# Mixer weights from 64-bit words: signs on GpSimd, group scales and norms by TensorE, new buffer choice

## The chip, the cores and the metric

The kernel runs on one core of one Trainium2 chip. The metric is the device time of one execution in microseconds (us), taken several times; beside it stands one profiled execution, whose trace gives the duration of each instruction. The engines are named as in the profile: PE is TensorE (matmuls), DVE VectorE, ACT ScalarE, POOL GpSimd, SP SyncE, which issues most DMA transfers.

## The reference, cut to what matters

Eight batches, 8 heads, 576 positions, head width 64. Attention is computed twice, once over positions pooled in fours and once in a band of seven positions, and the sum goes through a two-stage mixer, over tokens and over channels.

```python
x = attention_pooled(q, k, v) + attention_band(q, k, v)   # (8, 576, 512)
xt = x.transpose(0, 2, 1)
h = np.maximum(xt @ w_tok1, 0.0) @ w_tok2                 # 576 -> 256 -> 576
u = x + h.transpose(0, 2, 1)
h2 = np.maximum(u @ w_ch1, 0.0) @ w_ch2                   # 512 -> 1536 -> 512
return u + h2
```

The four weights arrive as 64-bit floating-point numbers, and the kernel makes them usable itself, once, while the first batch runs.

## The kernel before, in words

Each batch goes through the same steps. `pooled` (four pairs of heads: products sd, transposes td, products ad) and `local` (five tiles of positions: scores sc, transposes pT, products av) are the attention. `mix` is the token mixer: it splits x into two halves xh, multiplies by W1 (t1), splits the result (hid), multiplies by W2 with x added by transposing matmuls (t2), takes the largest magnitude (umx, and `everywhere`: a reduce um_m, a transpose um_t, a reduce um_m1, a broadcast um_b) and scales u into fp16 pairs uh. `first` is the channel mixer's first product (c1, twelve tiles for each of two chunks of 256 and 320 columns, three matmul passes each), `first_up` makes h of it, and `second` is the second product (c2). The columns of a batch's `second` and the next batch's attention and token mixer are interleaved.

The weights go through `to_f32` tile by tile. A raw tile has a high and a low 32-bit word for each element. ACT scales the high words (L175), POOL turns the low words into a small number (L178), DVE joins the two in one pass over two inputs (L180), and a second DVE pass, in `signed` (L184), puts the sign in and writes the tile to its place. For the token weights (W, nine tiles) ACT copies the upper part and DVE subtracts it (L215). For the channel weights (C1 and C2, twelve tiles of 128x512 each) PE multiplies the raw tiles by ones (C_sum, L279 and L288), DVE reduces (L283), and one scale comes out of all twelve tiles of a weight (`big`, `pow2`, L262); only then ACT writes the fp16 upper half of each tile (L268) and DVE the lower half (L270), which every product of `first` needs:

```python
    yield step("V", 0.6, *([("C1", NF - 1)] if self.at else []))
    nc.vector.tensor_reduce(big, self.mx[:, :self.n], axis=AX.X, op=ALU.max)
    pow2(big, 2.0 ** -self.k, self.inv, self.s)
```

Raw tiles of W and C1 share five buffers (`h`), those of C2 come in pairs in the two buffers `vw`. At the start POOL builds three masks and a pattern with many small selections, and adds the value rows (vr, L344 and L345) for the pooled attention.

The order of all this for the first batch, the weights and the first steps of the second batch is made by the list scheduler `drive`: streams yield steps with an engine, an assumed duration and needs, and the step that can begin earliest is written next (within PATIENCE, 0.3 us, the earlier stream wins). From the second batch on `main` writes a batch's channel products, and `tick` lets the next batch's other work (`side`) in between them at a fixed rate.

## Time and profile before

| what | value |
|---|---|
| runs | 975.58 to 978.17 us, median 976.34 of 3 |
| profiled execution | 977.24 us |
| its span, first to last instruction | 975.5 us |
| busy in the span | PE 907.9, DVE 506.0, ACT 301.1, POOL 112.4 us |
| granted TensorE clock, mean | 0.975 of full speed |

The profiled execution lies 0.90 us above the median, and its span 1.74 us below its own time. PE is busy 93% of the span, DVE 52%; these are means over stages with different limits. The first 110 us hold the attention and token mixer of batch 0 and most of the weights' preparation, and the rest is eight times the channel mixer with the next batch's other work in between. The profile's line for 40 equal slices shows PE at 5, 7, 4, 7, 7 tenths in the first five slices, and at 8 or 9 from there on.

### The profile page before, as it was taken

Reading aid. Unit: us, or ns where it says so; the run is one execution under the profiler, and the core shown is the slowest. Engines: PE = TensorE matmul, PEld = TensorE weight load, DVE = VectorE, ACT = ScalarE, POOL = GpSimd, SP = SyncE. Lnnn points to the kernel's source line nnn. Section 1 sums busy time; section 2 is a strip of 40 time slices with the busy share of each in tenths; the row PEclk is TensorE's granted clock in tenths of the full one; section 3 lists DMA queues with packets and bytes.
Section 4 is the critical chain, followed back from the end, with each engine's and each line's share of the span. In section 5 each row is a group of like instructions: output and inputs, shape, how many; then the busy total and the mean of one; then the engine's idle time right before and its main releaser. Section 6 shows DMA issues by size and latency. Waiting matters only on the chain. (4 is left out here: it accounts for less than half of the span.)

```text
span 975.5 us, 25542 instructions
## 1 busy us (share of the span) xinstructions
PE 907.9 (93%) x11292; PEld 712.2 (73%) x11292; DVE 506.0 (52%) x1187; ACT 301.1 (31%) x627; POOL 112.4 (12%) x213
## 2 busy tenths in 40 slices
PE   5747789999999999999999999999999999999998
PEld 4634467778867778677877778777876778777876
DVE  7879899244645354724555354724645345533221
ACT  1544456212323232422333232422432222322110
POOL 7143500030030003000120003000120000000000
PEclk9976799999999999999999999999999999999999
DMA  8266610530025002500133002600034000000000
GB/s 225 96 234 239 217 31 2 159 90 21 26 61 158 22 8 76 168 7 21 38 107 100 15 14 72 171 1 28 20 84 140 15 15 20 18 2 21 18 12 28
DMA packets 28221, 68.28 MB, mean 70 GB/s; under 512 B 3504, under 2 KB 14000, under 8 KB 26864
## 3 DMA queue, kind: packets, MB, share of 16 engines
q1 hardware_dynamic: 25552, 64.30, 21.9%
q10 hardware_dynamic: 2560, 2.36, 0.9%
q8 instruction: 88, 1.44, 0.6%
q14 instruction: 21, 0.17, 0.1%
HBM read 54.85 MB, written 9.44 MB: 66 GB/s over the span
## 5 line engine op out<-in xcount | busy, mean ns | idle before, releaser
L105 PEld LDWEIGHTS <-CW 128*128 128x128 f16 x4608 | 435.7, 98 | 136.5 <-issue 15.3
L105 PE MATMUL c<-uh,CW 128*128 128x256 f16 (+1 forms) x2304 | 310.7, 288 | 7.0 <-DVE CW L270 4.4
L105 PE MATMUL c<-h,CW 128*128 128x256 f16 (+1 forms) x2304 | 304.5, 287 | 0.8 <-issue 0.7
L646 DVE SCALAR_TENSOR_TENSOR h<-c,h 128x256 f16<-128x256 f32 (+1 forms) x192 | 87.3, 455 | 133.0 <-ACT h L644 131.9
L644 ACT ACTIVATE h<-c 128x256 f16<-128x256 f32 (+1 forms) x192 | 78.4, 408 | 211.2 <-PE c L105 211.0
L344 POOL TENSOR_TENSOR vr<-vr 72x256 f32<-72x256 f32 x64 | 49.0, 765 | 489.4 <-DMA vr<-in_vr_dram 298.1
L672 DVE SCALAR_TENSOR_TENSOR u<-c,io,u 128x256 f32<-128x256 f32 (+1 forms) x64 | 33.0, 516 | 109.7 <-PE c L105 109.7
L554 DVE TENSOR_REDUCE umx<-t 128x1 f32<-128x256 f32 (+1 forms) x64 | 29.2, 457 | 84.5 <-ACT u L552 84.4
L105 PE MATMUL t<-W,hid 128*128 128x256 f32 (+1 forms) x384 | 71.6, 323 | 0.0
L105 PE MATMUL t<-xh,W 128*128 128x512 f32 (+1 forms) x240 | 68.2, 419 | 1.1 <-ACT x L480 0.8
L552 ACT COPY u<-t 128x256 f32<-128x256 f32 (+1 forms) x64 | 25.5, 398 | 119.9 <-PE t L105 119.6
L105 PEld LDWEIGHTS t<-W,hid 128*128 128x128 f32 x384 | 56.7, 200 | 2.6 <-DVE hid L531 0.3
L105 PEld LDWEIGHTS t<-xh,W 128*128 128x128 f32 (+1 forms) x240 | 43.6, 192 | 12.5 <-issue 2.5
L475 PE MATMUL av<-vw,pt 47*32 47x64 f32 x2304 | 37.1, 233 | 14.6 <-ACT pt L466 4.4
L480 ACT COPY x<-av 128x512 f32<-128x512 f32 (+1 forms) x40 | 23.3, 582 | 88.4 <-PE av L475 80.9
L475 PEld LDWEIGHTS av<-vw,pt 47*32 47x32 f32 x2304 | 28.9, 110 | 25.2 <-issue 11.4
L567 ACT ACTIVATE uh<-u,us 128x256 f16<-128x256 f32 (+1 forms) x64 | 29.6, 524 | 49.0 <-DVE us L111 45.0
L407 PE MATMUL ad<-vd,ptd 72*72 72x65 f32 x512 | 42.5, 240 | 0.1
L407 PEld LDWEIGHTS ad<-vd,ptd 72*72 72x72 f32 x512 | 40.5, 157 | 1.3 <-ACT ptd L401 0.4
L545 PEld LDWEIGHTS t<-ident,x 128*128 128x128 f32 (+1 forms) x160 | 22.4, 146 | 18.4 <-issue 9.1
L545 PE MATMUL t<-ident,x 128*128 128x128 f32 (+1 forms) x160 | 33.0, 287 | 2.3 <-DVE umx L554 2.3
L569 DVE SCALAR_TENSOR_TENSOR uh<-u,us,uh 128x256 f16<-128x256 f32 (+1 forms) x64 | 31.1, 537 | 7.6 <-ACT uh L567 7.6
(84 smaller groups left out, 802.6 us busy)
## 6 DMA issues: line engine op xcount, KB each, us to landing
qk<-in_qk_dram SPq DMA_DIRECT2D x32, 579.0 KB
vw<-in_vw_dram SPq DMA_DIRECT2D x32, 351.0 KB
vr<-in_vr_dram SPq DMA_DIRECT2D x64, 144.0 KB
C_raw<-in_c_dram SPq DMA_DIRECT2D x12, 512.0 KB
C_raws<-in_c_dram SPq DMA_DIRECT2D x12, 512.0 KB
out_dram<-u SPq DMA_DIRECT2D x32, 160.0 KB
out_dram<-u SPq DMA_DIRECT2D x32, 128.0 KB
vw<-od ACTq DMA_DIRECT2D x32, 72.0 KB
```

The costliest lines, as they stand in the source:

```text
L105: nc.tensor.matmul(ps, lhs(a), rhs(c), start=first and i == 0, stop=last and i == 2, **kw)
L344: nc.gpsimd.tensor_add(t[:, 0:2], t[:, 0:2], t[:, 2:4])
L407: nc.tensor.matmul(ps[:, g, par], pt[:, par, kg, G * g:G * g + G], st.vd[:, kg, 2 * pr + par], start=kg == 0, stop=kg == 1)
L475: nc.tensor.matmul(ps[QB * j:QB * j + QB, par, D * hp:D * hp + D], pt[p, hp, QB * j:QB * j + QB], st.vw[h][p, g, D * hp:D * hp + D], start ...
L545: nc.tensor.matmul(ps[:, o:o + n], xf(t)[:, 128 * c:128 * c + 128], ident[:n, :n], start=i == 0, stop=False, is_transpose=True, skip_group ...
L552: nc.scalar.copy(u, ps)
L554: nc.vector.tensor_reduce(umx[:, c:c + 1], ps, axis=AX.X, op=ALU.max, apply_absolute_value=True)
L567: nc.scalar.activation(t[:, 0], us[c], AF.Copy, scale=s)
L569: nc.vector.scalar_tensor_tensor(t[:, 1], us[c], s, t[:, 0], ALU.mult, ALU.subtract)
L644: nc.scalar.activation(ht[:, 0], ps, AF.Relu)
L646: nc.vector.scalar_tensor_tensor(ht[:, 1], ps, 0.0, ht[:, 0], ALU.max, ALU.subtract)
L672: nc.vector.scalar_tensor_tensor(us[c], banks[c], io, us[c], ALU.mult, ALU.add)
```

## The change

- **Signs.** `to_f32` has a second POOL instruction per tile (L214, behind the first, now L211): it takes the high words and writes the upper 16 bits of the sign into the low word. DVE's one pass (L219) then joins shifted high word and low word and writes the tile to its place; `signed` is gone. SG=4 gives all 33 tiles' signs to POOL.
- **Norms and scales.** PE multiplies each finished tile by itself (L304 for C1, L323 for C2) in place of the product of ones and raw tile. C1 gets a scale for every four tiles (`First.scale`), so that the parts of a group (now L293) wait for that group alone. C2 has one scale, worked out from group norms that are multiplied by C1's constants (`Second.scale`).
- **Loads and buffers.** C1's raw tiles have six buffers of their own (`cw`, later C2's finished tiles), W's the five of `h`; C2's first four raw tiles use batch 0's `qk` buffers, the rest the pairs in `vw`. PSUM banks and the buffers `w` have a tag each, and `drive` picks the one that comes free first.
- **PE filler.** `keep_busy` writes matmuls of a constant tile, 14 at the start, and up to 8 ahead of a PE step for which the scheduler foresees a wait, until the second chunk's uh of batch 0; 88 of them stand ahead of batch 0's first c1 product, 22 of these ahead of the first sd.
- **Masks.** 10 selections and two copies in place of 26 and 8 selections; the pattern comes from a DVE reduce of the identity.
- **Mixer.** `mix` is four streams (splits, products, takes, scaled), which `together` interleaves with the next batch's attention start; `drive` runs until batch 0 is over and batch 1's first uh is made.

```diff
-PATIENCE = 0.3
+SG = 4
+PATIENCE = 0.0
...
+    def slot(k):
+
+        if not driven[0]:
+            now_in[k] = (now_in[k] + 1) % SLOTS[k]
+        return k + str(now_in[k])
...
-        return psum.tile([128, 512], F32, tag="m", name=name, bufs=3)
+        return psum.tile([128, 512], F32, tag=slot("m"), name=name, bufs=1)
...
+    for kind, j, base, step_ in ((0, 0, -3, 1), (2, 1, QB + 2, -1)):
+        nc.gpsimd.tensor_copy(masks[kind], m)
+        select(masks[kind][QB * j:QB * j + QB], base, 0, step_, WB, NEG)
...
+    def keep_busy(n):
+
+        if n:
+            ps = P1("busy")
+            for _ in range(n):
+                nc.tensor.matmul(ps, junk[:, :128], junk, start=True, stop=True)
...
+            if e == "P" and ("uh", 0, 1) not in made and free["g"]:
+                keep_busy(min(8, int((t - clock["P"]) * 0.6 / 0.22)))
...
+                i = now_in[k] = min(free[k], key=free[k].get)
+                del free[k][i]
...
+        top = raw.bitcast(BF16).rearrange("p (n four) -> p n four", four=4)[:, :, 1]
...
         nc.gpsimd.tensor_scalar(lo, lo, 2.0 ** -29, -0.501, ALU.mult, ALU.add)
-        yield step("V", 0.08 + n * 0.0012)
-        nc.vector.scalar_tensor_tensor(lo, hi, 3, lo, ALU.logical_shift_left, ALU.bitwise_or)
...
-    def signed(y, raw):
-        words = raw.rearrange("p (n two) -> p n two", two=2)
-        nc.vector.scalar_tensor_tensor(y, words[:, :, 1], 0x80000000, words[:, :, 0],
-                                       ALU.bitwise_and, ALU.bitwise_or)
...
+        if by_pool():
+            yield step("G", 0.08 + n * 0.0026)
+            nc.gpsimd.tensor_scalar(top, hi.bitcast(F32), 2.0 ** -126, 2.0 ** -126, ALU.mult, ALU.mult)
+        else:
+            yield step("V", 0.08 + n * 0.0015)
+            nc.vector.scalar_tensor_tensor(lo, hi, 0x80000000, lo, ALU.bitwise_and, ALU.bitwise_or)
+        e = yield step("V", 0.08 + n * 0.0012, *needs)
+        nc.vector.scalar_tensor_tensor(lo if y is None else y(), hi, 3, lo, ALU.logical_shift_left, ALU.bitwise_or)
+        return e
...
+    def weight_loads(pieces, tag, name):
         raws = {}
...
         for i, (src, n) in enumerate(pieces):
...
+            yield step("S", 0.1, *([(name, "read", i - BUFS[tag])] if i >= BUFS[tag] else []))
+            raws[i] = T([src.shape[0], 2 * n], U32, tag, f"{name}{i}_raw")
+            nc.sync.dma_start(raws[i], src)
+            made[name, "raw", i] = fetched(src.shape[0] * n * 8)
+            made[name, "raw"] = raws
...
+        def tile(self, i, *needs):
             name = self.name
...
+            yield step("A", 0.0, (name, "raw", i))
+            raw = made[name, "raw"][i]
+            e = yield from to_f32(raw, made[name, "raw", i], lambda: self.place[i + 1].bitcast(U32), *needs)
+            make((name, "read", i), e)
+            e = yield step("P", 0.5, *([(name, "y", i - 1)] if i else []), take="m>" + name if i % 4 == 0 else "")
+            make((name, "y", i), e)
+            self.sums(i, self.place[i + 1].bitcast(BF16).rearrange("p (n two) -> p n two", two=2)[:, :, 1])
...
+        def norms(self, q):
+
+            yield step("V", 0.68, (self.name, "y", 4 * q + 3), give="m>" + self.name)
+            nc.vector.tensor_reduce(self.mx[:, q:q + 1], self.banks[q], axis=AX.X, op=ALU.max)
+
+        def root(self, src, f, inv, s):
+
+            nc.vector.tensor_scalar(inv.bitcast(U32), src.bitcast(U32), 0x7F000000, 1, ALU.bitwise_and,
+                                    ALU.logical_shift_right)
+            nc.vector.tensor_scalar(inv, inv, 2.0 ** 64 * f, 2.0 ** -60 * f, ALU.mult, ALU.max)
+            nc.vector.reciprocal(s, inv)
...
+    class First(Channel):
+        def sums(self, i, ab):
+
+            if i % 4 == 0:
+                self.banks[i // 4] = PM(f"C1_sum{i}")
+            for d in range(4):
+                a = ab[:, 128 * d:128 * d + 128]
+                nc.tensor.matmul(self.banks[i // 4][:, 128 * (i % 4):128 * (i % 4) + 128], a, a, start=d == 0, stop=d == 3)
+
+        def scale(self):
+            for q in range(NQ):
+                yield from self.norms(q)
+                big = yield from everywhere(f"C1_n{q}", self.mx[:, q:q + 1])
+                e = yield step("V", 0.45, give="g")
+
+                self.root(big, 2.0 ** (4.5 + 0.5 - 8), self.inv[q], self.s[q])
+                make(("C1", "scale", q), e)
+                for i in range(4 * q, 4 * q + 4):
+                    yield from self.parts(i)
...
+            big = yield from everywhere("C2_n", self.mx)
+            yield step("V", 0.9, give="g")
+
+            self.root(big, 2.0 ** (4.5 + 2 + 0.5 - 14), ic, self.s[0])
+            for q in reversed(range(NQ)):
+                nc.vector.tensor_mul(self.s[q], self.s[0], C1.inv[q])
...
+        def loads(self):
+
+            self.raws = made["C2", "raw"] = []
             for i in range(NF):
...
+                if i < 4:
+                    yield step("S", 0.1, *(("tile", 0, t) for t in range(len(TILES))))
+                    t = T([128, S + KW], F32, "qk", f"C2_raw{i}")[:, :1024].bitcast(U32)
+                else:
+                    if i % 2 == 0:
+                        yield step("S", 0.1, *(("av", 0, t) for t in range(len(TILES))), *([("C2", "read", i - 4), ("C2", "read", i - 3)] if i >= 8 else []))
+                        two = T([128, 2, 1024], U32, "vw", f"C2_raws{i}")
+                    t = two[:, i % 2]
+                nc.sync.dma_start(t, u32(c2[i]))
+                self.raws.append(t)
+                made["C2", "raw", i] = fetched(2 ** 19)
...
-    def sums_c1(w, i, ab):
-
-        if i % 4 == 0:
-            w.bank = PM(f"C1_sum{i}")
-        for d in range(4):
-            nc.tensor.matmul(w.bank[:, 128 * (i % 4):128 * (i % 4) + 128], onesb, ab[:, 128 * d:128 * d + 128],
-                             start=d == 0, stop=d == 3)
...
-            yield step("V", 0.6, *([("C1", NF - 1)] if self.at else []))
-            nc.vector.tensor_reduce(big, self.mx[:, :self.n], axis=AX.X, op=ALU.max)
-            pow2(big, 2.0 ** -self.k, self.inv, self.s)
...
+        return [splits(), products(), takes(), scaled()]
...
             m = mix(st)
             if b + 1 < B:
-                yield from together([m, ahead(b + 1)], 2)
-            else:
-                yield from m
+                m.append(ahead(b + 1))
+            yield from together(m, len(m))
...
+        keep_busy(14)
...
+        streams = [x for k in "LMUSCTDWmPaAHQh" for x in group[k]]
+        left = drive(streams, [("over", 0, 1)] + [("uh", 1, 0)] * (B > 1))
```

`parts` is the old loop of upper and lower halves, with the scale of the tile's group.

Where the instructions stand is shown at three places. The first is POOL, from its first weight tile (W10 and W0 are the first tile of W1, C10 the first of C1; W20 is the first of W2 before). Before:

```order
L178 TENSOR_SCALAR W10_raw_244<-W10_raw_244 128x256
L178 TENSOR_SCALAR C10_raw_248<-C10_raw_248 128x512
L178 TENSOR_SCALAR W11_raw_246<-W11_raw_246 128x256
L178 TENSOR_SCALAR W20_raw_253<-W20_raw_253 128x288
L178 TENSOR_SCALAR W12_raw_522<-W12_raw_522 128x256
L178 TENSOR_SCALAR W13_raw_711<-W13_raw_711 128x256
L178 TENSOR_SCALAR W21_raw_255<-W21_raw_255 128x288
L178 TENSOR_SCALAR C11_raw_250<-C11_raw_250 128x512
```

After the change, from the same point:

```order
L211 TENSOR_SCALAR W0_raw_199<-W0_raw_199 128x256
L214 TENSOR_SCALAR W0_raw_199<-W0_raw_199 128x256
L211 TENSOR_SCALAR C10_raw_207<-C10_raw_207 128x512
L211 TENSOR_SCALAR W1_raw_209<-W1_raw_209 128x256
L214 TENSOR_SCALAR C10_raw_207<-C10_raw_207 128x512
L214 TENSOR_SCALAR W1_raw_209<-W1_raw_209 128x256
L211 TENSOR_SCALAR C11_raw_211<-C11_raw_211 128x512
L211 TENSOR_SCALAR W2_raw_213<-W2_raw_213 128x256
L214 TENSOR_SCALAR C11_raw_211<-C11_raw_211 128x512
L214 TENSOR_SCALAR W2_raw_213<-W2_raw_213 128x256
```

Each tile has two instructions in place of one, and W's and C1's tiles alternate. 28 such pairs (8 of W, 20 of 128x512) stand between C10's L211 and the last raw tile whose join stands on DVE ahead of the first c1 product.

The second place is DVE ahead of what batch 0's first c1 product waits for. Before, that is the lower half CW0 of C1's first tile (the last row shown is the row ahead of it and one more):

```order
L569 SCALAR_TENSOR_TENSOR uh0_1_0_1267<-u0_1_0_1170,us0_1_1258,uh0_1_0_1267 128x320
L262 TENSOR_REDUCE C1_big_1269<-C1_mx_252 128x1
L109 TENSOR_SCALAR C1_inv_1270<-C1_big_1269 128x1
L110 TENSOR_SCALAR C1_inv_1270<-C1_inv_1270 128x1
L111 RECIPROCAL C1_s_1271<-C1_inv_1270 128x1
L569 SCALAR_TENSOR_TENSOR uh0_1_1_1274<-u0_1_1_1196,us0_1_1258,uh0_1_1_1274 128x320
L184 SCALAR_TENSOR_TENSOR CW22_198<-C28_raws_1109 128x512
L569 SCALAR_TENSOR_TENSOR uh0_1_2_1281<-u0_1_2_1213,us0_1_1258,uh0_1_2_1281 128x320
L270 SCALAR_TENSOR_TENSOR CW0_176<-CW1_177,C1_s_1271,CW0_176 128x512
L569 SCALAR_TENSOR_TENSOR uh0_1_3_1286<-u0_1_3_1235,us0_1_1258,uh0_1_3_1286 128x320
```

After, it is the last uh of the first chunk (the last row here); CW0 to CW7 are done, and CW8 and CW9 too:

```order
L282 TENSOR_SCALAR C1_inv2_123<-C1_n2_b_1337 128x1
L284 TENSOR_SCALAR C1_inv2_123<-C1_inv2_123 128x1
L285 RECIPROCAL C1_s2_126<-C1_inv2_123 128x1
L648 SCALAR_TENSOR_TENSOR uh0_0_1_1340<-u0_0_1_1174,us0_0_1309,uh0_0_1_1340 128x256
L219 SCALAR_TENSOR_TENSOR CX3_1179<-C2_raws6_1026 128x512
L293 SCALAR_TENSOR_TENSOR CW8_142<-CW9_143,C1_s2_126,CW8_142 128x512
L648 SCALAR_TENSOR_TENSOR uh0_0_2_1360<-u0_0_2_1201,us0_0_1309,uh0_0_2_1360 128x256
L219 SCALAR_TENSOR_TENSOR CX4_1180<-C2_raws6_1026 128x512
L293 SCALAR_TENSOR_TENSOR CW9_143<-CW10_144,C1_s2_126,CW9_143 128x512
L648 SCALAR_TENSOR_TENSOR uh0_0_3_1374<-u0_0_3_1221,us0_0_1309,uh0_0_3_1374 128x256
```

Ahead of the first c1 product DVE now has 29 passes L219 where it had 31 L180 and 31 L184; it has ten lower halves (L293) where it had one (L270), four of uh (of the first chunk) where it had seven (four of the first, three of the second chunk), and three group chains where there was one for all twelve tiles.

The third place is DVE where batch 1 ends and batch 2 begins (u1_1 is batch 1's output of its second chunk, the others belong to batch 2's mixer). Before:

```order
L488 TENSOR_REDUCE um2_0_m_4226<-umx2_0_4114 128x1
L672 SCALAR_TENSOR_TENSOR u1_1_2_2910<-c2_1_1_2_4174,io1_1_4034,u1_1_2_2910 128x320
L494 TENSOR_REDUCE um2_0_m1_4230<-um2_0_t_4228 1x1
L109 TENSOR_SCALAR ui2_0_4234<-um2_0_b_4232 128x1
L110 TENSOR_SCALAR ui2_0_4234<-ui2_0_4234 128x1
L111 RECIPROCAL us2_0_4235<-ui2_0_4234 128x1
L569 SCALAR_TENSOR_TENSOR uh2_0_0_4252<-u2_0_0_4124,us2_0_4235,uh2_0_0_4252 128x256
L569 SCALAR_TENSOR_TENSOR uh2_0_1_4255<-u2_0_1_4147,us2_0_4235,uh2_0_1_4255 128x256
L569 SCALAR_TENSOR_TENSOR uh2_0_2_4258<-u2_0_2_4173,us2_0_4235,uh2_0_2_4258 128x256
L569 SCALAR_TENSOR_TENSOR uh2_0_3_4261<-u2_0_3_4209,us2_0_4235,uh2_0_3_4261 128x256
L554 TENSOR_REDUCE umx2_1_4264<-t2_2_1_0_4265 128x1 x2
```

After:

```order
L751 SCALAR_TENSOR_TENSOR u1_1_1_2964<-c2_1_1_1_4276,io1_1_4192,u1_1_1_2964 128x320
L629 TENSOR_REDUCE umx2_1_4422<-t2_2_1_0_4326 128x1 x2
L751 SCALAR_TENSOR_TENSOR u1_1_2_2991<-c2_1_1_2_4336,io1_1_4192,u1_1_2_2991 128x320
L629 TENSOR_REDUCE umx2_1_4422<-t2_2_1_2_4373 128x1 x2
L557 TENSOR_REDUCE um2_0_m1_4442<-um2_0_t_4440 1x1
L551 TENSOR_REDUCE um2_1_m_4486<-umx2_1_4422 128x1
L118 TENSOR_SCALAR ui2_0_4449<-um2_0_b_4447 128x1
L119 TENSOR_SCALAR ui2_0_4449<-ui2_0_4449 128x1
L120 RECIPROCAL us2_0_4450<-ui2_0_4449 128x1
L648 SCALAR_TENSOR_TENSOR uh2_0_0_4471<-u2_0_0_4241,us2_0_4450,uh2_0_0_4471 128x256
L751 SCALAR_TENSOR_TENSOR u1_1_3_2997<-c2_1_1_3_4408,io1_1_4192,u1_1_3_2997 128x320
L648 SCALAR_TENSOR_TENSOR uh2_0_1_4477<-u2_0_1_4289,us2_0_4450,uh2_0_1_4477 128x256
```

Both reduces of the second chunk (umx2_1) have moved ahead of the first chunk's scale, and batch 1's last output u1_1_3 now stands between uh2_0_0 and uh2_0_1. On PE, um2_0_b has 57 matmuls behind it ahead of the first c1 of batch 2 before, and 9 now; for batches 3 to 6 these are 110 to 140 before and 22 to 26 now.

## Rows read from the trace of the kernel before

**Rows 1.** Stages: PE, PEld, DVE, ACT, POOL busy (instructions), clock, DMA share, GB/s.

```profile
29.20:110.20 81.00, 52.13 (x654) 37.79 (x652) 67.58 (x134) 35.38 (x74) 23.90 (x34) 0.78 0.57 206
110.20:171.00 60.80, 54.32 (x714) 40.52 (x715) 57.74 (x122) 34.76 (x65) 13.73 (x17) 0.93 0.15 33
...
200.00:975.50 775.50, 757.13 (x9216) 597.09 (x9214) 349.27 (x857) 216.28 (x464) 57.19 (x101) 1.00 0.17 49
```

**Rows 2.** PE's timeline: start, duration, instruction, idle before and releaser.

```profile
110.20 0.61 PE L105 MATMUL c<-uh,CW 128*128 128x256 f16 x2 [2.31 <-ACT CW L268]
112.30 2.74 PE L105 MATMUL c<-uh,CW 128*128 128x256 f16 x12 [1.49 <-DVE CW L270]
```

**Rows 3.** DVE's waits from 29.2 to 110.2: total us, times, longest.

```profile
DVE umx L554 <- ACT u L552: 3.9, 2, 2.8
DVE W_raw L180 <- POOL W_raw L178: 3.4, 2, 3.0
DVE hid L531 <- ACT hid L529: 2.0, 1, 2.0
```

**Rows 4.** DVE's groups by form in the same stretch: count, busy, mean ns.

```profile
L184 DVE SCALAR_TENSOR_TENSOR CW<-C_raw 128x512 uint32<-128x512 uint32 x12 | 9.4, 781 | 0.2
L180 DVE SCALAR_TENSOR_TENSOR C_raw<-C_raw 128x512 uint32<-128x512 uint32 x12 | 9.0, 752 | 0.9 <-POOL C_raw L178 0.9
...
L184 DVE SCALAR_TENSOR_TENSOR W_raw<-W_raw 128x288 uint32<-128x288 uint32 x4 | 1.8, 454 | 0.1
...
L569 DVE SCALAR_TENSOR_TENSOR uh<-u,us,uh 128x320 f16<-128x320 f32 x2 | 1.1, 541 | 0.0
```

**Rows 5.** DVE's timeline in stretches where POOL does nothing.

```profile
62.52 0.69 DVE L180 SCALAR_TENSOR_TENSOR C_raws<-C_raws 128x512 uint32<-128x512 uint32 x1
...
126.36 0.74 DVE L270 SCALAR_TENSOR_TENSOR CW<-CW,C_s,CW 128x512 f16<-128x512 f32 x1
```

**Rows 6.** POOL's timeline around its first weight tiles.

```profile
12.80 0.72 POOL L344 TENSOR_TENSOR vr<-vr 72x256 f32<-72x256 f32 x1
13.60 0.46 POOL L345 TENSOR_TENSOR vd<-vr 72x128 f32<-72x128 f32 x1
...
27.24 0.42 POOL L178 TENSOR_SCALAR W_raw<-W_raw 128x256 uint32<-128x256 uint32 x1 [6.98 <-DMA W_raw<-in_w_dram]
29.15 0.64 POOL L178 TENSOR_SCALAR C_raw<-C_raw 128x512 uint32<-128x512 uint32 x1 [1.49 <-DMA C_raw<-in_c_dram]
```

**Rows 7.** POOL's groups by form from 0 to 110.2: count, busy, mean ns.

```profile
L178 POOL TENSOR_SCALAR C_raw<-C_raw 128x512 uint32<-128x512 uint32 x12 | 9.4, 787 | 15.2 <-DMA C_raw<-in_c_dram 14.9
```

**Rows 8.** The ten us behind the first c1 product, columns as in group 1.

```profile
110.20:120.20 10.00, 7.84 (x39) 4.82 (x39) 9.05 (x12) 5.16 (x10) 9.53 (x12) 0.60 0.45 109
```

**Rows 9.** The timeline there, all engines.

```profile
111.30 0.95 DVE L270 SCALAR_TENSOR_TENSOR CW<-CW,C_s,CW 128x512 f16<-128x512 f32 x1
111.65 1.17 POOL L344 TENSOR_TENSOR vr<-vr 72x256 f32<-72x256 f32 x1
...
113.96 1.21 DVE L270 SCALAR_TENSOR_TENSOR CW<-CW,C_s,CW 128x512 f16<-128x512 f32 x1
```

**Rows 10.** PE's timeline where batch 0 ends and batch 1 begins.

```profile
227.51 0.38 PE L497 MATMUL um_b<-um_m,ones 1*128 1x1 f32 x2
...
229.57 0.39 PE L105 MATMUL c<-uh,CW 128*128 128x256 f16 x2
```

**Rows 11.** DVE's timeline there.

```profile
226.30 0.55 DVE L672 SCALAR_TENSOR_TENSOR u<-c,io,u 128x320 f32<-128x320 f32 x1 [0.63 <-PE c L105]
226.77 0.27 DVE L494 TENSOR_REDUCE um_m<-um_t 1x1 f32<-1x128 f32 x1
...
228.31 0.16 DVE L111 RECIPROCAL us<-ui 128x1 f32<-128x1 f32 x1
...
229.28 1.68 DVE L569 SCALAR_TENSOR_TENSOR uh<-u,us,uh 128x256 f16<-128x256 f32 x4
```

**Rows 12.** One c2 product's matmuls in PE's timeline.

```profile
442.67 3.43 PE L105 MATMUL c<-h,CW 128*128 128x320 f16 x24
```

More of the change, by code (lines that the diff above doesn't have):

```diff
@@ L11 @@
 U32 = mybir.dt.uint32
+U16 = mybir.dt.uint16
 U8 = mybir.dt.uint8
@@ L111, in pow2 @@
         nc.vector.reciprocal(s, inv)
-    clock = dict.fromkeys("AGVPSD", 0.0)
+    clock = dict(A=2.0, G=5.0, V=2.0, P=0.0, S=0.0, D=0.0)
     now = [0.0]
-    free = dict(gg=[0.0] * 2, m=[0.0] * 3, g=[0.0], w=[0.0] * 4)
+    free = {k: {i: 0.0 for i in range(n)} for k, n in SLOTS.items()}
+    held = {}
     made = {}
@@ L166, in drive, with by_pool, to_f32 @@
                 it[1] = None
+        driven[0] = False
+        for k, n in SLOTS.items():
+            first = min(free[k], key=free[k].get) if free[k] else [i for (x, _), v in held.items() for i in v if x.split(">")[0] == k][0]
+            now_in[k] = (first - 1) % n
         return [it for it in items if it[1] is not None]
-    def to_f32(raw, at):
+    count = [0]
+    def by_pool():
+        count[0] += 1
+        return count[0] * SG % 4 < SG
+    def to_f32(raw, at, y=None, *needs):
         n = raw.shape[1] // 2
@@ new lines, in token_weight @@
+    def token_weight(i, n, f):
+        yield step("A", 0.0, ("W", "raw", i))
+        raw = made["W", "raw"][i]
+        yield from to_f32(raw, made["W", "raw", i])
+        y = raw.rearrange("p (n two) -> p n two", two=2)[:, :, 0].bitcast(F32)
+        yield step("A", 0.1 + n * 0.0011)
+        nc.scalar.copy(f[:, 0], y)
+        e = yield step("V", 0.08 + n * 0.0012)
+        nc.vector.tensor_tensor(f[:, 1], y, f[:, 0].bitcast(F32), ALU.subtract)
+        make(("W", "y", i), e)
+        make(("W", "read", i), e)
@@ L431, in local @@
         one = "m" if b == 0 else "g"
-        yield step("P", 0.7, ("q", b, 3), *([("tile", b, t - 3)] if t > 2 else []), take="gg")
+        yield step("P", 1.0, ("q", b, 3), *([("tile", b, t - 3)] if t > 2 else []), take="gg")
         ps = P2(f"sc{b}_{t}")
@@ new lines, in splits @@
+        def splits():
+            for t in range(NT):
+                n = TILES[t][1]
+                yield step("A", 0.62, ("x", b, t), *([("over", 0, 0)] if b == 1 else []),
+                           *([("t1", b, t - 3)] if t > 2 else []))
+                xh = st.xh[t] = T([n, 2, 512], F32R, "xh", f"xh{b}_{t}")
+                nc.scalar.copy(xh[:, 0], xf(t))
+                e = yield step("V", 0.69)
+                nc.vector.tensor_tensor(xh[:, 1], xf(t), xh[:, 0].bitcast(F32), ALU.subtract)
+                make(("xh", b, t), e)
@@ L600, in ahead @@
     def ahead(b):
-        yield step("S", 0.1, *([("mixed", 0)] if b == 1 else []))
+        yield step("S", 0.1, *([("C2", "read", i) for i in range(4)] + [("pair", 0, 3)] if b == 1 else []))
         st = load(b)
@@ L608, in ahead @@
         if b == 1:
-            yield step("S", 0.1, ("C2", "rough"))
+            yield step("S", 0.1, *(("C2", "read", i) for i in range(4, NF)))
             load_w(st)
@@ L679, in through, with second_weights @@
             yield from g
-    def scale_out():
-        yield step("V", 0.1, ("C2", NF - 1))
-        nc.vector.tensor_mul(ic, C1.inv, C2.inv)
     def main(st, places):
         banks = [], []
-        up = through(first_up(st, 0), first_up(st, 1), scale_out(), second_up(st, 0, banks[0]),
-                     second_up(st, 1, banks[1]))
-        return [up, through(first(st, 0, places[0]), first(st, 1, places[1]),
-                            second(st, 0, banks[0]), second(st, 1, banks[1]))]
+        up = [first_up(st, 0), first_up(st, 1), through(second_up(st, 0, banks[0]), second_up(st, 1, banks[1]))]
+        return up, [first(st, 0, places[0]), first(st, 1, places[1]),
+                    through(second(st, 0, banks[0]), second(st, 1, banks[1]))]
+    def second_weights():
+        yield step("S", 0.0, *(("C1", "read", i) for i in range(NF)))
+        C2.place = pairs("CX") + singles(1, "CY")
+        make(("C2", "places"), now[0])
+        yield from C2.scale()
     def lazily(what, *needs):
@@ L700, in attend, with mix_of @@
                 + [lazily(lambda t=t: local(ready[b], t), ok) for t in range(len(TILES))])
+    mixes = {}
+    def mix_of(b):
+        if b not in mixes:
+            mixes[b] = mix(ready[b])
+        return mixes[b]
     def windows(st):
```

355 lines of the change are left out of this document (161 added, 194 removed).

## The prediction

> **What bounds the kernel now.** I read the busy time by stage first, then the instruction that ends the first stage, then what it waits for. From 200 us on PE is busy 757.13 of 775.50 us at full clock [rows 1]; at most 18 us are to be had there, and the change takes no product out of it. From 29.2 to 110.2, PE is busy only 52.13 of 81.00 us, at a granted clock of 0.78, while DVE has 67.58 us of work [rows 1]. The reader is to see that this stretch ends with batch 0's first c1 product at 110.20, which waited for a part of C1 from ACT, and that the next products wait for DVE's lower halves [rows 2]. All products come behind that one, so its start, T1, moves the end one for one, as long as nothing later is late. DVE sets T1: its work there, what stretches that work, and its idle 81.00 - 67.58 = 13.4 us.
>
> **The DVE work ahead of T1.** The order has 33 weight passes fewer there (62 of L180 and L184 before, 29 of L219 now): 9 on W tiles and 24 on channel tiles. A 128x512 pass with POOL at rest takes 0.69 us [rows 5], one on a W tile about 0.44 (0.454 for 128x288 in company [rows 4]). So 24 x 0.69 + 9 x 0.44 = 20.5 us go. Nine more lower halves come ahead of the first product (ten, where there was one), at 0.74 each [rows 5]: +6.7. They are no loss in all, since they go from behind T1 to ahead of it. Three uh of the second chunk go behind, at 0.54 [rows 4]: -1.6. Three group chains instead of one, of small operations of 0.16 and 0.27 us [rows 11], a first reduce of C2's norms and the pattern's reduce, less the second chunk's own small chain that goes behind: +2.2. Sum: -20.5 + 6.7 - 1.6 + 2.2 = **-13.2 us**, before any stretching.
>
> **DVE's idle time.** Of the 13.4 us, 3.4 are raw W tiles late from POOL [rows 3] and 0.9 raw C tiles [rows 4]. With six buffers of their own, C1's tiles are requested before the attention needs anything more, and POOL works ahead; I count these as gone, and 1 us more, as passes ready to run fill other waits. The waits for ACT in the token mixer (3.9 and 2.0 [rows 3]) are latencies of a chain that the change leaves, and stay. **-5.4 us**; bounds -1.4 (new waits for POOL take their place) and -10.4 (3 us are left).
>
> **What POOL's new work does to DVE.** L214 has no row. It reads 512 words and writes 512 halves, one input. The nearest row is L178, 128x512, one input: 0.64 alone [rows 6]. From the other side, POOL's sums of two inputs took 0.46 at 128 elements and 0.72 at 256 [rows 6], 0.26 per 128, so 0.72 + 2 x 0.26 = 1.24 at 512. It writes two bytes with a step of eight, and converts; I take y = 1.0, between the two, and 0.6 for a W tile. POOL then has 20 x (0.79 + 1.0) + 8 x (0.5 + 0.6) = 45 us (0.787 is L178 in company [rows 7]; W by 0.42 alone [rows 6] and as much stretching) between 29.2 and T1. Started at 29.2 this is done by 74, 25 us ahead of T1 as summed below, so POOL itself is no bound.
>
> But it is busy 45 of 70 us, 0.63, where it was busy 23.90 of 81, 0.30 [rows 1], and DVE is stretched by POOL: the passes took 0.781 and 0.752 in this stretch [rows 4] where 0.69 is the time alone [rows 5], +0.08. Where POOL was busy 9.53 of 10 us [rows 8], two lower halves took 0.95 and 1.21 [rows 9] for 0.74 alone [rows 5], +0.34 in the mean. DVE has some 63 passes with two inputs ahead of T1 now, and had 75, stretched by 75 x 0.08 = 6 us in all. By the first row in proportion to POOL's share, 63 x 0.08 x 0.63 / 0.30 = 10.6, so +5; by the second, 63 x 0.34 x 0.63 / 0.95 = 14.2, so +8; by the worst row (0.47) at every pass, 29.6, so +24. If L214 takes 0.64, the share is 0.53 and the first reading gives +3. I take **+8 us**, the higher of the two proportional readings, since that row has the denser POOL; bounds +3 and +24.
>
> The Trainium skill ("SBUF — State Buffer", section "Who interferes with whom") says that a DVE instruction with two SBUF inputs contends with a GpSimd instruction that reads SBUF, and that the shared ports are an exclusive lock, held for the whole instruction. The stretched rows above agree with it on both engines. Taken as a wait for the whole other instruction at each pass it would put the sum near the bound of +24, and that is a rival below. The same skill ("GPSIMD Engine Reference", section "Engine selection") has one-input elementwise work on GpSimd at about line rate and advises VectorE for elementwise work; by the first half L214 would be near L178 and the sum some 5 us lower.
>
> T1 = 110.2 - 13.2 - 5.4 + 8 = **99.6**, that is -10.6.
>
> **Behind T1.** From 110.2 to 171 PE is idle 60.80 - 54.32 = 6.5 us [rows 1], the first part of it in waits for lower halves [rows 2], and its first 10 us run at a clock of 0.60 [rows 8]: with 7.84 us busy, 3.1 us of that are clock. Now ten lower halves are done when the products begin, DVE has some 10 us less to do in this stretch, and POOL's value sums of batch 1 still come there. Against it: second-chunk uh, the remaining joins of C2 and all its lower halves lie there, and c2 waits for a scale from all C2 tiles. I take **-4 us** of the 9.6; bounds 0 and -8.
>
> **Filler matmuls.** 88 of 512 columns, at most 0.25 us each, are 22 us of PE, inside the 28.9 us that PE is idle ahead of T1 [rows 1]. Up to 8 in a row can stand ahead of a real step, 2 us; what hides this is that DVE, not PE, ends the stretch. The 22 ahead of the first sd run while the inputs load. I take 0. If the cover is gone, each wrong guess of the scheduler costs up to 2 us; this is inside the bounds on idle time.
>
> **Masks, buffers, loads.** 22 small POOL operations fewer at the start lie ahead of value sums that wait for their transfer: 0. The norm products on PE are as many matmuls as before for C1, and four for one for C2, 36 more short ones in PE's idle time: 0.
>
> **The batch boundaries.** At batch 1's start, um_b ended at 227.89 and the first c1 product began at 229.57 with no wait shown, ten matmuls lying between [rows 10]; DVE needs two more small operations, 0.16 each, and the first uh, 0.42 of four in 1.68 [rows 11]. At batch 2 now only nine matmuls lie between, eight of them of 0.143 us (3.43 for 24 [rows 12]), and the output u1_1_3 (0.55 [rows 11]) stands between the first uh and the second, behind the last c2 product. PE has 3 c1 matmuls, some 0.4 us, to bridge about 1.2. For batch 2 that is +0.5 for the first and +0.7 for the second: **+1.2 us**. Batches 3 to 6 have 22 to 26 matmuls, 3.1 us or more, between um_b and c1; at batch 1 the last uh was ready 3.1 us after um_b [rows 10, 11], and the first product needs only the first of them to begin: 0. Bounds 0 and +12 (2 us at each of six boundaries).
>
> **Sum.** 977.24 - 10.6 - 4.0 + 1.2 = 963.8 for the profiled execution; that one lies 0.90 above the median of the runs, so **963 us**.
>
> **The rivals.**
> 1. *Early.* L214 is as cheap as L178, DVE's stretching is +5 and its idle falls to 3: T1 = 110.2 - 13.2 - 10.4 + 5 = 91.6; with -8 behind it, 977.24 - 18.6 - 8 - 0.9 = 950. For it: POOL has work ready at all times now. Against: the ACT waits of the mixer's chain have no cause to go. 0.15.
> 2. *The lock eats it.* Every two-input pass is stretched as the worst row: +24, T1 = 115.6, and 977.24 + 5.4 - 4 + 1.2 - 0.9 = 979; half way there, 971. For it: the row of 1.21 [rows 9]. Against: it fell where POOL did sums of 1.17 us on end, twice as long as L178. 0.12, most of it within 0.3%.
> 3. *GpSimd becomes the bound* (slower). POOL's work ahead of T1 is 20 x (0.79 + y) + 8 x (0.5 + 0.55 y) = 19.8 + 24.4 y. It is ready at 49.0 + 24.4 y; this passes 99.6 at y = 2.1 and 110.2 at y = 2.5, if writing single halves is that slow. At y = 3, joins, norm and lower half behind the last tile give T1 about 124, and 977.24 + 13.8 - 4 + 1.2 - 0.9 = 987. Nothing in the rows is that slow. 0.08.
> 4. *The boundaries eat it.* The scale chains, now behind both chunks' reduces, cost 2 us at each of six boundaries: 963 + 11 = 974. Against: 22 to 26 matmuls of cover at most of them. 0.05.
>
> **The numbers.** The forecast has 0.60, with its own range 953 to 972, from -5 and +4 in idle time, -5 and +6 in stretching, and 4 behind T1. About 0.3% (2.9 us) is what a measurement of this kernel can tell from no change. Faster by more than that (under 973.4): the forecast's 0.57, rival 1's 0.15, some of rivals 2 and 4, 0.76 in all; within it 0.14, from rivals 2 and 4 and the forecast's tail; slower 0.10, rival 3 and the tail of rival 2. The range 948 to 978 leaves out rival 3, half of rival 2 and the tail of rival 1.
>
> **What would show it.** The first c1 product near 99.6 (92 to 108). L219 at 0.80 to 0.95 us; under 0.78 speaks for rival 1, over 1.1 for rival 2. L214 on 128x512 near 1.0 us, and POOL done with C1 by 75; if DVE waits for L214 in long pieces up to T1, rival 3. DVE busy some 62 of 70 us between 29.2 and T1. PE's idle time in the 60 us behind T1 near 3 us; PE waits for uh at batch 2 near 1 us and none at batches 3 to 7. The prediction is wrong if DVE does not end the stretch: if the first product waits for a PE chain (transposes or norms behind filler), or for raw tiles by DMA.

## The result, and the profile after

The changed kernel takes 966.66 us (median of 4 runs, 964.95 to 968.17), against 976.95 for the kernel before in the same comparison: a ratio of 0.9895, interval 0.9872 to 0.9917. The time lies in the likeliest case's own range; the forecast of 963 is 3.7 us low. The profiled execution took 967.21 us, with a span of 965.3.

The busy time by stage, cut at T1 and at the same distances behind it as in [rows 1] (columns as there):

```profile
29.20:107.90 78.70, 58.17 (x688) 37.56 (x687) 62.57 (x120) 41.57 (x83) 62.20 (x55) 0.85 0.56 185
107.90:168.70 60.80, 57.39 (x892) 45.22 (x890) 51.54 (x120) 30.70 (x62) 20.34 (x25) 1.00 0.24 65
168.70:197.70 29.00, 28.79 (x367) 23.15 (x368) 14.89 (x34) 6.64 (x12) 1.93 (x3) 1.00 0.56 168
197.70:965.30 767.60, 752.14 (x9175) 589.80 (x9173) 344.44 (x851) 215.67 (x462) 54.77 (x99) 1.00 0.17 49
```

The one stage of before that is not in [rows 1]:

```profile
171.00:200.00 29.00, 27.45 (x480) 22.67 (x479) 10.58 (x26) 6.59 (x12) 0.00 (x0) 0.94 0.59 165
```

TensorE's timeline has the first c1 product here, with no wait in its first 24 matmuls (two waits before [rows 2]):

```profile
107.92 2.78 PE L114 MATMUL c<-uh,CW 128*128 128x256 f16 x24
```

T1 has moved by 2.3 us, from 110.2 to 107.9, not by 10.6. Behind it the span is 857.4 us, where it was 865.3: 7.9 us less. TensorE's idle time behind T1 is 3.4 + 0.2 + 15.5 = 19.1 us, and was 6.5 + 1.6 + 18.4 = 26.4. So most of the gain shows behind T1, where the forecast had 2.8. One part of it is a wait of TensorE in the 60.8 us behind T1 of before:

```profile
PE c L105 <- DVE CW L270: 4.4, 5, 1.5
```

After the change no product waits for a lower half, and the granted clock is 1.00 in the two stages behind T1, where it was 0.93 and 0.94. Of the 7.3 us of idle time that are gone, 2.9 lie from 197.7 on.

VectorE ends the stretch, as forecast: its last uh begins at 107.23 and takes 0.47 us, and the first product starts at 107.92, behind two filler matmuls. VectorE's busy time ahead of T1 from 29.2 on, 62.57 us, is as forecast (62); its idle time is 78.70 - 62.57 = 16.1 us, forecast as 8, 13.4 before. GpSimd is busy 62.20 us where 45 was forecast; it was to be done with C1 by 75, and VectorE's join of C1's last tile begins at 85.06.

VectorE's waits from 29.2 to 107.9 (total, times, longest):

```profile
DVE CW L219 <- POOL C_raw L214: 4.1, 4, 1.8
DVE r L519 <- ACT P L516: 3.5, 1, 3.5
DVE W_raw L219 <- POOL W_raw L214: 2.1, 3, 0.7
...
DVE CX L219 <- POOL C_raw L214: 1.4, 2, 0.9
```

Its groups by form in the same stretch, and GpSimd's (count, busy, mean ns, idle before):

```profile
L293 DVE SCALAR_TENSOR_TENSOR CW<-CW,C_s,CW 128x512 f16<-128x512 f32 x10 | 11.5, 1148 | 0.8 <-ACT CW L291 0.8
L219 DVE SCALAR_TENSOR_TENSOR CW<-C_raw 128x512 uint32<-128x512 uint32 x12 | 10.4, 867 | 4.1 <-POOL C_raw L214 4.1
L219 DVE SCALAR_TENSOR_TENSOR CX<-C_raw 128x512 uint32<-128x512 uint32 x4 | 3.6, 910 | 1.4 <-POOL C_raw L214 1.4
```

```profile
L214 POOL TENSOR_SCALAR C_raw<-C_raw 128x512 bf16<-128x512 f32 x16 | 24.3, 1518 | 10.9 <-ACT C_raw L208 9.8
L211 POOL TENSOR_SCALAR C_raw<-C_raw 128x512 uint32<-128x512 uint32 x15 | 13.0, 867 | 1.2
```

The reader is to see that the joins, which waited 4.3 us for GpSimd's first pass before [rows 3, 4], now wait 7.6 us for L214; that the join is stretched to 0.867 and the lower half to 1.148 (0.69 and 0.74 alone [rows 5]); and that L214 takes 1.518 us, half as much again as the 1.0 taken, and more than the upper bound of 1.24. The first L214 runs while VectorE is idle or has short operations, so that its time is near the time alone. GpSimd's timeline:

```profile
32.51 1.36 POOL L214 TENSOR_SCALAR C_raw<-C_raw 128x512 bf16<-128x512 f32 x1 [3.59 <-ACT C_raw L208]
```

At the batch boundaries no product waits for uh; TensorE's waits from 168.7 to the end:

```profile
PE av L538 <- DMA vw<-od: 4.4, 4, 1.9
PE td L461 <- ACT pd L454: 3.8, 6, 0.8
PE pT L525 <- DVE P L521: 3.1, 6, 1.4
PE t L602 <- ACT u L627: 0.4, 1, 0.4
```

One stall is new, and the profile names no releaser for it. TensorE's timeline:

```profile
17.74 0.86 PE L470 MATMUL ad<-vd,ptd 72*72 72x65 f32 x10
22.61 0.87 PE L470 MATMUL ad<-vd,ptd 72*72 72x65 f32 x6 [4.00 <-issue]
```

### The profile page after: what moved, and what is told of

Its sections match the earlier page's. It is cut to its first block, busy times and chain, and to the rows that moved or that the text cites. A ratio compares the mean times of both kernels' runs of the same rounds, so it can differ in the third digit from the quotient of the medians.

```text
span 965.3 us, 25834 instructions
## 1 busy us (share of the span) xinstructions
PE 919.2 (95%) x11433; PEld 708.9 (73%) x11433; DVE 493.8 (51%) x1174; ACT 300.8 (31%) x627; POOL 154.4 (16%) x221
## 5 line engine op out<-in xcount | busy, mean ns | idle before, releaser
L114 PE MATMUL c<-h,CX 128*128 128x256 f16 (+1 forms) x2304 | 306.9, 286 | 0.0
L114 PEld LDWEIGHTS <-CW 128*128 128x128 f16 x2304 | 216.0, 98 | 68.1 <-issue 15.1
L114 PEld LDWEIGHTS <-CX 128*128 128x128 f16 x2304 | 216.4, 98 | 58.5 <-issue 1.5
L629 DVE TENSOR_REDUCE umx<-t 128x1 f32<-128x256 f32 (+1 forms) x64 | 29.2, 457 | 86.4 <-ACT u L627 68.4
L114 PE MATMUL t<-W,hid 128*128 128x256 f32 (+1 forms) x384 | 67.1, 310 | 0.0
L114 PEld LDWEIGHTS t<-W,hid 128*128 128x128 f32 x384 | 53.1, 188 | 2.2
L470 PE MATMUL ad<-vd,ptd 72*72 72x65 f32 x512 | 39.1, 229 | 4.3 <-issue 4.0
L470 PEld LDWEIGHTS ad<-vd,ptd 72*72 72x72 f32 x512 | 37.2, 146 | 5.8 <-issue 4.6
L509 DVE TENSOR_TENSOR P<-sc,mask 128x304 f32<-128x304 f32 (+1 forms) x40 | 18.7, 468 | 30.7 <-PE sc L502 30.7
L151 PE MATMUL busy<-junk 128*128 128x512 bf16 x93 | 31.4, 469 | 3.2 <-DVE junk L84 1.6
```

The lines of the kernel that those rows point to most:

```text
L114: nc.tensor.matmul(ps, lhs(a), rhs(c), start=first and i == 0, stop=last and i == 2, **kw)
L151: nc.tensor.matmul(ps, junk[:, :128], junk, start=True, stop=True)
L470: nc.tensor.matmul(ps[:, g, par], pt[:, par, kg, G * g:G * g + G], st.vd[:, kg, 2 * pr + par], start=kg == 0, stop=kg == 1)
L629: nc.vector.tensor_reduce(umx[ch][:, c:c + 1], ps, axis=AX.X, op=ALU.max, apply_absolute_value=True)
```

## The experiments

Each is the changed kernel with one edit. Where an edit touches the scheduler's steps, the first batch's order is made anew. The ratio is to the kernel before, run beside it; T1 is from the run's own trace. Two runs whose intervals overlap are not told apart.

| run | T1 | median us | ratio, interval |
|---|---|---|---|
| before | 110.2 | 976.95 | |
| changed kernel | 107.9 | 966.66 | 0.9895, 0.9872 to 0.9917 |
| sg0_signs_on_dve | 115.7 | 970.31 | 0.9922, 0.9896 to 0.9948 |
| sg2_half_the_signs | 126.9 | 974.49 | 0.9973, 0.9955 to 0.9990 |
| no_filler | 104.0 | 965.06 | 0.9870, 0.9848 to 0.9892 |
| late_c1_loads | 101.7 | 965.62 | 0.9871, 0.9837 to 0.9905 |
| c2_joins_behind_uh | 102.0 | 961.12 | 0.9849, 0.9819 to 0.9880 |
| scale_after_all_c1 | 107.0 | 970.91 | 0.9941, 0.9921 to 0.9962 |
| old_mixer_order | 106.9 | 966.12 | 0.9891, 0.9865 to 0.9917 |
| filler_late_only | 106.1 | 960.58 | 0.9838, 0.9819 to 0.9857 |
| no_sign_work | 96.8 | 952.04 | 0.9739, 0.9710 to 0.9768 |
| filler_late_c2_behind | 100.5 | 960.83 | 0.9822, 0.9798 to 0.9845 |
| filler_late_c2_all_behind | 97.2 | 962.49 | 0.9833, 0.9809 to 0.9857 |
| signs_by_act_filler_late | 115.9 | 966.94 | 0.9896, 0.9878 to 0.9915 |

**Who makes the signs.**

```diff
-SG = 4
+SG = 0
```

> The changed kernel with all 33 signs made by a second VectorE pass instead of GpSimd, all else as changed (the list scheduler orders anew). Theory A, GpSimd holds the first c1 product (it is busy 62 of the 79 us ahead of it, and VectorE waits 7.6 us for sign instructions): VectorE gets 29 passes back ahead of it, +18 us, and loses about 7 us of stretching and 7 us of waits, so the first c1 product is at 108 to 113 and the time 967 to 972. Theory B, moving the signs off VectorE is the gain: +15 us or more, 978 to 985. A time under 964 would say that the sign move costs more than it brings.

970.31 us, as theory A had it, with T1 later than it said (115.7 for 108 to 113). The move to GpSimd brings some 3.7 us, not 15, and as this interval overlaps the changed kernel's, even that is not clear of the scatter. With the signs still on VectorE the kernel is at 0.9922 of before, so the larger part of the gain comes from the rest of the change. VectorE's groups by form up to 107.9, with the sign pass at L217:

```profile
L217 DVE SCALAR_TENSOR_TENSOR C_raw<-C_raw 128x512 uint32<-128x512 uint32 x16 | 11.6, 728 | 1.9 <-ACT C_raw L208 1.9
L293 DVE SCALAR_TENSOR_TENSOR CW<-CW,C_s,CW 128x512 f16<-128x512 f32 x12 | 8.9, 739 | 0.8 <-ACT CW L291 0.8
L219 DVE SCALAR_TENSOR_TENSOR CW<-C_raw 128x512 uint32<-128x512 uint32 x12 | 8.1, 676 | 0.0
```

Without L214 the lower half is at its time alone (0.739 for 1.148) and the join too (0.676 for 0.867): it is L214 that stretches them, for the most part (no_sign_work below keeps some of the lower half's stretching).

```diff
-SG = 4
+SG = 2
```

> The changed kernel with every second sign made by VectorE and the others by GpSimd. Theory A (GpSimd holds the first c1 product): VectorE +9 us of passes, -6 us of waits and -6 us of stretching, time 962 to 966. Theory B (VectorE's work alone counts): +7 us, 972 to 975.

974.49 us, slower than either end; theory A fell here, and B had the size. VectorE's busy time from 0 to 960 us is 500.5 us, as with no sign on GpSimd (500.9), while all signs on GpSimd give 493.2: what the moved half saved, stretching took. The new order's T1 of 126.9 is the latest of all; which of its steps makes it so late was not settled.

```diff
-            nc.gpsimd.tensor_scalar(top, hi.bitcast(F32), 2.0 ** -126, 2.0 ** -126, ALU.mult, ALU.mult)
```

> The changed kernel without the 33 sign instructions of GpSimd, the order of everything else unchanged; this leaves the signs of the weights out, so its output is not the reference's. It prices L214, which took 1.52 us where 1.0 was forecast. Theory A, GpSimd is what holds the first c1 product (62 of 79 us busy): 39 us of its work go, VectorE's waits for signs (7.6 us) and half of the stretching of its passes go, the first c1 product is at 95 to 99 and the time 955 to 959. Theory B, the written order of TensorE, ScalarE and VectorE holds it, and L214 costs little: first product at 104 to 106, 963 to 965.

952.04 us: L214 costs 14.6 us, more than theory A gave, at an unchanged order of everything else, and T1 is at 96.8, as it said. The run leaves the signs out, so it tells of time alone. GpSimd is busy 23.13 us from 29.2 to T1. The joins (L218 here) are no longer stretched, and wait for nothing; the lower half still takes 0.847 us for 0.74 alone, and no run shows by what. VectorE's groups up to 107.9:

```profile
L292 DVE SCALAR_TENSOR_TENSOR CW<-CW,C_s,CW 128x512 f16<-128x512 f32 x12 | 10.2, 847 | 0.8 <-ACT CW L290 0.8
L218 DVE SCALAR_TENSOR_TENSOR CW<-C_raw 128x512 uint32<-128x512 uint32 x12 | 8.3, 694 | 0.0
```

```diff
...
-            yield step("G", 0.08 + n * 0.0026)
-            nc.gpsimd.tensor_scalar(top, hi.bitcast(F32), 2.0 ** -126, 2.0 ** -126, ALU.mult, ALU.mult)
+            yield step("A", 0.1 + n * 0.0011)
+            nc.scalar.activation(top, hi.bitcast(F32), AF.Copy, scale=2.0 ** -126)
```

The lines left out are the two of filler_late_only, shown below.

> The changed kernel with only the late filler and with the signs written by ScalarE (the same two bytes per element, one multiplication) in place of GpSimd's L214; the order is made anew. ScalarE is busy 42 of the 79 us ahead of the first c1 product and gets some 17 us more (29 passes of about 0.65 and 0.43, by its scaling passes of the same tiles). Theory A, L214 costs by GpSimd's own time and by stretching VectorE, so that another engine with room does it better: GpSimd is busy under 30 us there, VectorE's join takes 0.70 to 0.75 and the lower half 0.75 to 0.85, first c1 product at 95 to 102, 951 to 957. Theory B, ScalarE's queue becomes the late one (its passes stand between the mixer's copies, for which VectorE and TensorE wait): 958 to 964.

966.94 us, against 960.58 for the same filler with the signs on GpSimd (filler_late_only). The signs do not arrive in this run: its output is as far from the reference as that of no_sign_work (a relative error of 7745.76 in both), so it tells of time alone. Theory A had VectorE nearly right (join 0.758, just over its range; lower half 0.783), and B went further than it said: ScalarE is busy 64.25 of 76.80 us up to 106, because the same two-byte write takes it 1.351 us, where it scales a tile in 0.700. ScalarE's groups up to 107.9:

```profile
L214 ACT ACTIVATE C_raw<-C_raw 128x512 bf16<-128x512 f32 x16 | 21.6, 1351 | 6.9 <-DMA vw<-od 6.9
L208 ACT ACTIVATE C_raw<-C_raw 128x512 f32<-128x512 f32 x16 | 11.2, 700 | 0.0
L291 ACT ACTIVATE CW<-CW,C_s 128x512 f16<-128x512 f32 x12 | 8.5, 706 | 0.1
```

The last line is the upper half of a finished tile: it writes two bytes per element too, but side by side, and takes no longer than the four-byte write. So the two bytes alone are not what costs. The step of eight bytes is left, or the product itself, which is so small that nothing but a sign is to remain; no run parts these two.

**The filler.**

```diff
-        if n:
+        if n < 0:
```

> The changed kernel without the 102 filler matmuls, the order of everything else unchanged. Theory A, the filler pays by the clock: the granted clock ahead of the first c1 product falls to 0.7 to 0.8 and the first products behind it run at 0.6, as before the change: 969 to 972. Theory B, the filler is neutral or in the way (TensorE is not what ends the stretch, and a stall of 4.0 us at 18.6 lies behind filler): 963 to 967, and the stall gone if filler caused it.

965.06 us: B by the median, though its interval overlaps that of the changed kernel; the granted clock fell as A had it (0.71 from 60 to 100, 0.87 in the changed kernel, and the first 24 c1 matmuls took 4.63 us for 2.78). The stall is gone. The next run has the late filler alone.

```diff
-            if e == "P" and ("uh", 0, 1) not in made and free["g"]:
+            if e == "P" and ("uh", 0, 1) not in made and free["g"] and t > 40:
...
-        keep_busy(14)
```

> The changed kernel with only the filler matmuls that the scheduler places behind 40 us of its own clock (40 of 102), the rest of the order unchanged. Theory A, the early filler causes TensorE's stall of 4.0 us near 18.6, in which nothing is recorded, and the late filler only keeps the clock up: no such stall, first c1 product at 103 to 105, its first 24 matmuls in about 2.8 us, 962.5 to 964.5. Theory B, both are neutral within the scatter: 965 to 967, with the stall still there or its time lost elsewhere.

960.58 us, better than both theories' ranges, and clear of the changed kernel's interval: to leave out the early filler is worth some 6 us, and the late filler brings some 4.5 against none (these two intervals overlap a little, the single runs do not). T1 is later than A had it (106.1). A stall without a releaser is still there, later and shorter; TensorE's timeline of this run:

```profile
21.25 0.47 PE L502 MATMUL sc<-qk 64*32 64x38 f32 x22
24.05 0.73 PE L502 MATMUL sc<-qk 64*32 64x38 f32 x42 [2.33 <-issue]
```

In this run and in the changed kernel 222 recorded matmuls lie ahead of the stall, though the instruction that stalls is another one (sc here, ad there). So it is in all the runs here but no_filler (221 recorded in no_sign_work), for 2.3 to 5.9 us. The transfers in the traces show what goes with it. Each time a 16 KB transfer on the queue that the profile calls instruction (q8) ends 1.3 to 1.6 us before TensorE resumes: at 21.04 in the changed kernel (TensorE resumes at 22.61), at 22.70 here (24.05), at 23.40 in sg0_signs_on_dve (25.03). In no_filler it ended at 19.02, 2.4 us before TensorE came to that place, and there is no stall, though the same 222 matmuls lie ahead as here. So, as far as timing can show it, TensorE stood still for its next instructions and not for anything in its data, and the stall depends on when that transfer ends. What makes it late, while the transfer engines are at a share of 0.92 up to 29.2 us in the changed kernel, was not tested.

So early filler is not what causes the stall. It puts real work behind it (36 of the 222 matmuls are filler in the changed kernel, none here), and the first sd starts at 8.48 us behind 22 filler matmuls, where it starts at 6.00 here. T1 is only 1.8 us earlier here. Of the 6.3 us between the two spans, 3.1 are waits of TensorE for the pooled outputs' transfers from 195.9 and 197.7 on (1.3 us here, 4.4 in the changed kernel), where the two programs do the same; old_mixer_order, with all the early filler, has 1.1 us of them. So the time that early filler costs is shown by the runs, and most of its way there is open.

**Loads, scales and order.**

```diff
-            yield step("S", 0.1, *([(name, "read", i - BUFS[tag])] if i >= BUFS[tag] else []))
+            yield step("S", 0.1, *([(name, "read", i - BUFS[tag])] if i >= BUFS[tag] else []),
+                       *([("pair", 0, 3)] if name == "C1" and i > 1 else []))
```

> The changed kernel with C1's raw tiles from the third on requested only behind the last pooled pair of batch 0 (the order is made anew). Theory A, the prefetched tiles hold back the small transfers of the pooled output (issued at 39.4, the last 45.2, while ScalarE's queue stands still 6.1 us): that wait falls under 2 us, the first c1 product comes 4 to 8 us earlier, 961 to 965. Theory B, the raw tiles are late instead, as they were before the change: GpSimd and VectorE wait for them, 967 to 972.

965.62 us, no difference from the changed kernel, and between the two theories' ranges. T1 came 6 us earlier, and the end did not. ScalarE's issue of the four pooled outputs takes 5.62 us here and 5.78 in the changed kernel (3.44 before). This does not clear the prefetched tiles: the edit puts five requests for C1 at 34.25 to 39.99, just ahead of that issue at 41.03, and the transfer engines are at a share of 0.84 during it (0.73 in the changed kernel, 0.33 before). Whether tiles in flight hold the issue up is thus not tested.

```diff
             for q in range(NQ):
                 yield from self.norms(q)
+            for q in range(NQ):
                 big = yield from everywhere(f"C1_n{q}", self.mx[:, q:q + 1])
```

> The changed kernel in which C1's scales are worked out only when all twelve tiles' norms are there (group scales as values, but the old wait). Theory A, the group wait is what lets ten lower halves be done ahead of the first c1 product: without it these come behind, the products wait for them as before the change, TensorE is idle 3 to 5 us more behind the first product, and the time is 969 to 972. Theory B, the same VectorE work only changes places: 965 to 968.

970.91 us, the time that theory A gave, and clear of the changed kernel's interval: at nearly the same T1 (107.0) the group scales are worth 4.3 us. Its mechanism is not what the trace shows. One lower half is done ahead of T1, where ten were, and yet no product waits for one; TensorE's idle time behind T1 is 16.0 us (19.1 in the changed kernel). What has grown is its busy time there, 844.2 us for 838.3, at a granted clock of 0.95 and 0.87 in the stages of 60.8 and 29 us behind T1, where the changed kernel has 1.00. Why the clock fell there was not tested.

```diff
...
-            m = mix(st)
+            m = mix_old(st)
             if b + 1 < B:
-                m.append(ahead(b + 1))
-            yield from together(m, len(m))
+                yield from together([m, ahead(b + 1)], 2)
...
```

`mix_old`, left out here, is the mixer of the kernel before, written as one stream.

> The changed kernel with the token mixer of batches 2 to 7 written as one stream in the old order (norm chain of the first chunk between the chunks). Theory A, the four streams bring the 2.9 us that TensorE is idle less from about 198 us on: 969 to 970.5, TensorE idle some 18 us there. Theory B, that difference has another cause, or is scatter: 966 to 967.5.

966.12 us, theory B: the order at the boundaries is worth nothing measurable.

```diff
-        group["D"] = [C2.tile(i, ("C2", "places")) for i in range(NF)]
+        group["D"] = [C2.tile(i, ("C2", "places"), *([("uh", 0, 0)] if i > 2 else [])) for i in range(NF)]
```

> The changed kernel in which C2's tiles from the fourth on are joined on VectorE only behind batch 0's first uh (the order is made anew). Theory A, the start of the first c1 product is set by VectorE's written order, which has eight C2 joins ahead of it, and what is moved behind it is given back there: the product starts 3 to 5 us earlier (103 to 105), TensorE's idle time behind it grows by as much, and the time is 965 to 968. Theory B, the start of that product moves the end one for one: 962 to 963.5.

961.12 us, below both ranges, with an interval that touches the changed kernel's. By the medians the time fell by 5.5 us as T1 came 5.9 us earlier: here the end moved with T1, as theory B had it. With the early filler gone, the same edit was tried again, and then for all of C2 (`*([("uh", 0, 0)] if i > 2 else [])` becomes `("uh", 0, 0)`):

> The changed kernel with only the late filler and with C2's joins from the fourth on behind batch 0's first uh. If the two gains (some 6 and 5.5 us) have separate places, the stall at the start and the order ahead of the first c1 product: 955 to 958, first product at 100 to 103. If they are the same time, gained twice: 960 to 961.5.

> As the run before it, with all of C2's joins behind batch 0's first uh. If the start of the first c1 product moves the end one for one further on: 2 us less than the run before. If C2's joins now come late for c2's scale, TensorE waits between c1 and c2 and it is the same or 1 to 4 us more.

960.83 and 962.49 us: T1 goes from 106.1 to 100.5 and 97.2, and the time stays (960.58). The expectation of the same time gained twice holds for the first, and a rise of 1 to 4 us for the second, within the scatter. TensorE's idle time in the 89.8 us behind T1 grows from 3.3 us to 4.3 and 7.5. The lowest median with all signs is filler_late_only's, 960.58 us, but these two and c2_joins_behind_uh are not told apart from it.

## Why the prediction was right, step by step

- **VectorE's work ahead of T1** (-13.2, stretching +8): right in sum, 62.57 us for 62. Join 0.867 to 0.910, inside 0.80 to 0.95. The runs without L214 show that most of the stretching is L214's.
- **L214 at y = 1.0**: mis-sized. 1.36 us with little beside it and 1.52 in company; GpSimd 62.20 us for 45. Both bounds were rows that write four bytes per element; L214 writes two bytes with a step of eight and leaves nothing but a sign, and the same operation takes as long on ScalarE. All of L214 costs 14.6 us. Rival 3 (GpSimd becomes the bound) was not the outcome, for VectorE's longest wait for L214 is 1.8 us, but a part of its mechanism is there: 7.6 us of such waits.
- **Idle time -5.4**: failed, by sign: +2.7. Against the 4.3 us of waits for late tiles before there are 7.6 us of waits for L214 now; 3.5 us are for ScalarE, which stood behind its issue of the pooled outputs.
- **T1 = 99.6, and the end moves with it one for one**: T1 failed, by 8.3 us, nearly all of it the idle time (+2.7 for -5.4 is 8.1). That the end moves with it is not a rule. It followed where work was taken out (no_sign_work: T1 -11.1, time -14.6). Where the order alone moved T1, it followed at most once (c2_joins_behind_uh: -5.9, time -5.5, with intervals that touch) and otherwise not (late_c1_loads: -6.2, time -1.0; filler_late_c2_all_behind against filler_late_only: -8.9, time +1.9, inside the scatter). In the last of these TensorE is idle 4.2 us more behind T1: preparation was left to do there.
- **Behind T1, -4**: right in direction, and -7.9 in all from T1 to the end, near the lower bound of -8. The mechanism that was forecast is there: the 4.4 us of waits for lower halves are gone, and the granted clock is 1.00 behind T1. But 2.9 us less idle time lie from 197.7 on, where the forecast had +1.2; the mixer's new order is not their cause (old_mixer_order), and no run shows what is. That the group scales gain their 4.3 us by ready lower halves is not shown either (scale_after_all_c1).
- **Boundaries +1.2**: 0. No product waits for uh, and the old order is no faster. (Rival 1's 950 leaves this +1.2 out, which the other sums have; with it, it is 951.)
- **Filler 0**: right as a sum (-1.6 without it, inside the scatter), wrong as a reason: about 6 us lost early and 4.5 gained late. The 22 ahead of the first sd were to run while the inputs load; they took 6.97 us, 0.32 each for at most 0.25 in the prediction, and the first sd began 2.4 us later than without them (8.48 for 6.06 in no_filler).

The terms missed in opposite ways: T1 was forecast 8 us too early, and the gain behind it 5 us too small. That the sum held within 4 us is luck.

The Trainium skill ("SBUF — State Buffer", section "Who interferes with whom") has a two-input VectorE instruction contend with a GpSimd one that reads SBUF; the joins and lower halves agree (0.676 and 0.739 without L214, 0.867 and 1.148 with it), yet the stretching is 4.1 us on ten lower halves and 3.0 on sixteen joins shown, not a whole other instruction at each pass. The Trainium skill ("GPSIMD Engine Reference", section "Engine selection") has one-input elementwise work on GpSimd at about line rate; L178 at 0.64, beside VectorE's join of the same size at 0.69, agrees with it, and L214 at 1.36 does not.

## What to carry to other kernels

Price a moved operation by a row of its own form, output and result included, not only by its inputs and size: this one cost twice the nearest row on two engines, and most of what VectorE gained went there. When one engine prepares work for another, count the work that must be done before the steady part, not only the moment at which the first product starts: to reorder for an earlier start gained once at most, and to take work out gained more than the start showed. Try early and late filler apart: here one cost time and the other gained it, and the sum hid both. Where an engine stalls without a releaser, look in the trace for a transfer of instructions that ends just before it resumes.
